# Calls, a doubled rest and a lag: three small moves in an attention and gated-MLP kernel

## The chip, the cores and the metric

The kernel runs on one core of one Trainium2 chip. The metric is the device time of one execution in microseconds (us), the median of several runs. TensorE (PE in the profile) multiplies matrices into PSUM, VectorE (DVE) and ScalarE (ACT) do the elementwise work, GpSimd (POOL) and SyncE (SP) mostly issue transfers (DMAs) here.

## The reference, cut to what matters

All numbers are 32-bit floats, with S = 2048 tokens and D = 576 features.

```python
qkv = layernorm(x) @ wqkv                  # 32 heads of 18 features, split into q, k, v
for each token s, head h:                  # a window of 8 keys, two tokens apart
    att = softmax(q[s] . k[s - 2*w] * 18**-0.5 for w in range(8))   # masked below token 0
    o[s] = sum(att[w] * v[s - 2*w])
h = x + o @ wo
g, u = layernorm(h) @ w_gate, layernorm(h) @ w_up       # 4608 features each
out = h + (sigmoid(g) * u) @ w_down
```

## The kernel before, in words

**Blocks and groups.** The tokens are cut in four blocks of 512: block b holds the even (0, 1) or odd (2, 3) tokens of one half of the sequence. A block is four tiles of 128 tokens (NS = 4). The heads are cut in four groups g of eight heads (CG = 144 features). Most products are done in split precision: an operand is split into a high half (copied by ACT with rounding, line 104) and a low half (the difference, taken by VectorE, line 105), and three products of halves are added (`tok_major`, `prod`).

**The 576 features** are handled as four chunks of 128 and a rest of 64. The rest is doubled: columns 512 to 575 are copied to columns 576 to 639 (DX = 640), the doubled rest is transposed as one tile of 128 (`tr_rest`, line 150), and `split_rest` makes the upper 64 rows the low half (lines 108 and 109). A plain tile without that copy of the rest has D = 576 columns. The copy is called the twin here.

**QKV calls.** `qkv(b, g, ...)` is one call: four passes, one a tile, of 14 matmuls each (lines 157 to 160), each evicted by ACT (line 403). After the last pass ACT issues three stores: q, k and v of that block and group go to device memory (lines 407 and 409), and `emitted` notes (b, g). The split weights of a group, `w[g]`, live in two buffers (tag "qw"): `w[2]` takes the place of `w[0]`, `w[3]` that of `w[1]`, so the splits of `w[3]` have to wait for the last call that uses `w[1]`. `heads(order, ws, n)` runs a list of calls, and between two passes it lets the attention advance by n steps.

**Attention units.** `attention(at, b, g, o)` is one unit, all on VectorE but for one exponential: SP loads q, the keys kw and the values vw with their windows (lines 176 to 178), then come two multiplies of 128x2304 (line 189) and two reductions (line 193) for the logits, the softmax (lines 198 to 207), and two more multiplies with their additions (lines 215 to 226). A unit ends with o for its group: for block 0 it lies in a tile in the core, for blocks 1 to 3 POOL stores it to device memory (`oscr`, line 228), and with the last group a second, small store adds the twin (line 230). `att_all` runs the units of blocks 0 and 1 in the order (0,0), (0,1), (1,0), (0,2), (0,3), (1,1), (1,2), (1,3); a unit waits until its call has been emitted. After (0, 3) four copies make the twin of block 0's o (line 428) and `ready` is set.

**The front.** `proj_j` is the output projection of one tile: it transposes o (lines 146 and 150), splits it, multiplies by wo, adds h (line 262), normalizes and transposes again. `front` does this for block 0, in between the last calls, (2, 3) and (3, 3): after two passes of (2, 3) come its first two steps, the transposes and splits of all four tiles. The blocks 1, 2 and 3 get the same later, in the background of the MLP (`proj_scr`), with o loaded back from device memory (`oj`, `load_j`, line 956) in tiles of DX columns.

**The MLP.** A loop over weight blocks (`items`) does the gate and up products, for block 0 first alone (12 items, "std") and then for two blocks at a time with seven products in place of eight ("pair"), and the down products (lines 864 and 926). Background work (`bg_step`) is stepped in between, and a queue of down units is stepped by `units`. The attention of blocks 2 and 3 is such background work.

**The tail.** For the last weight blocks, `load_tails` loads the sums of the down products back from memory (lines 1232 and 1235), lets seven steps pass (`lag(7)`), and adds three pairs of them on VectorE (line 1240), one in each of the next steps, each issued behind the last addition (`added[0]`) of the pair at work: s1 (line 825) before step 1, s3 (line 839) before step 4, s2 (line 844) before step 5.

**What sets the order.** Each engine runs its instructions in one fixed order. The build makes it from the order in which the program is written, a model of times, and priorities: `high_priority` moves what is in its block forward. `tc.issue_after(x)` puts the instructions of its block behind x on x's engine. A tile's buffer is reused when those who read it are done.

Of the kernel before, what the change touches and what calls it, by code (L numbers as in the profile page):

```python
# [15 lines left out]
F32 = mybir.dt.float32  # L16
F32R = mybir.dt.float32r
AF = mybir.ActivationFunctionType
ALU = mybir.AluOpType
# [41 lines left out]
def kernel(ctx, tc, x, wqkv, wo, wmlp, out):  # L61
# [29 lines left out]
    qscr = [[dr.tile([P, NS * CG], F32, name=f"q{b}_{g}") for g in range(NG)] for b in range(4)]  # L91
    oscr = {b: dr.tile([P, NS, DX], F32, name=f"o{b}") for b in (1, 2, 3)}
    hacc = [dr.tile([P, NS, D], F32, name=f"h{b}") for b in range(2)]
# [6 lines left out]

    splits = []

    def split(hi, lo, src):
# [3 lines left out]
    def split_rest(t, src):  # L107
        act.activation(t, src, AF.Copy)
        dve.tensor_tensor(t[64:128], src[64:128], f32(t[64:128]), ALU.subtract)  # L109

# [57 lines left out]
    def attention(at, b, g, o):  # L168
# [17 lines left out]
        for u in range(2):  # L186
            us = slice(2 * u, 2 * u + 2)
            pr = at.tile([P, 2, W, CG], F32, name="pr")
            dve.tensor_tensor(pr, both(kw, u), q[:, us].unsqueeze(2).broadcast_to([P, 2, W, CG]),  # L189
                              ALU.mult)  # L190
            yield
            yield
            dve.tensor_reduce(lg[:, us].rearrange("p j w h -> p (j w h)"),  # L193
                              pr.rearrange("p j w (h d) -> p (j w h) d", d=DH),
                              AX.X, ALU.add)
            yield
# [30 lines left out]
        if spill:  # L227
            pool.dma_start(oscr[b][:, :, g * CG:(g + 1) * CG], o)
            if g == NG - 1:
                pool.dma_start(oscr[b][:, :, D:DX], o[:, :, CG - DR:CG])  # L230

# [14 lines left out]

    def proj_j(bank, t, wos, th, tl, xn_tile, put, order=(0, 1)):
        oj = t[0]
        pv = tr_main(bank(), oj)
        with tc.high_priority(HI):  # L250
            split(th[:, 0:4], tl, pv)
        yield
# [160 lines left out]
    o = None  # L413
    emitted = set()
    ready = []
    passes = []

    def att_all():
        nonlocal o
        for b, g in ((0, 0), (0, 1), (1, 0), (0, 2), (0, 3), (1, 1), (1, 2), (1, 3)):  # L420
            while (b, g) not in emitted:
                yield
            if o is None:
                o = tok_tile()
            yield from attention(at, b, g, None if b else o[:, :, g * CG:(g + 1) * CG])
            if (b, g) == (0, 3):
                for j in range(NS):
                    dve.tensor_copy(o[:, j, D:DX], o[:, j, DM:D])
                ready.append(b)

# [154 lines left out]
    pads(2)  # L585
    heads(((2, 1), (3, 1)), w, 2)
    w.append(qkv_w(3, wr))
    pads(3)
    h = load_x(0)
    wos = [None, wo_w(1, swo.tile([P, 2, 5, DH2], F32R, tag="wo", name="wo1"))]  # L590
    heads(((0, 2), (0, 3), (1, 2), (2, 2), (3, 2)), w, 2)
    wos[0] = wo_w(0, saw.tile([P, 2, 5, DH2], F32R, tag="qw", bufs=2, name="wow"))
# [61 lines left out]
    with tc.issue_after(getattr(last, "ins", last)):  # L654
        for _ in range(2):
            next(fr)
    for b in (2, 3):
        for j, _ in enumerate(more if b == 2 else qkv(b, 3, T[b], w[3])):
# [294 lines left out]
    def load_j(pj, b, j, i):  # L953
        e, hf = BLOCKS[b]
        t = pj.tile([P, D if i else DX], F32, bufs=NS, name="hj" if i else "oj")
        paced(t, (xv[e, hf] if i else oscr[b])[:, j])
        return t

    def proj_scr(pj, b, raw, wos, ins=None, after=None):
# [3 lines left out]
        def tile_j(t, j):  # L963
# [11 lines left out]

            yield from proj_j(bg_bank, t, wos, th[:, :, js], tl[:, :, js], lambda: t[0], put, (1, 0))

# [244 lines left out]
    def load_tails():  # L1222
# [145 lines left out]
```

## Time and profile before

| what | us |
|---|---|
| median of 3 runs | 1581.41 (1580.72 to 1584.34) |
| the profiled execution | 1584.01 |
| its span, from the first to the last instruction | 1582.2 |
| TensorE busy | 1551.0 |
| VectorE busy | 1255.2 |
| ACT busy | 879.2 |
| POOL busy | 199.9 |

A line of the timeline reads: start, duration, engine, line of the kernel, operation, tile written <- tiles read, shapes, count, and in brackets the idle time of the engine before it with what ended it. A line of the waits reads: who waited for whom, us in total, times, the longest. A line of the chain of work that ended last reads: start, duration, what. A line of the windows reads: the window, its length, busy time and count of TensorE's matmuls, its weight loads, VectorE, ACT and POOL, then the clock granted to TensorE as a share of full speed, the busy share of the DMA engines and GB/s.

### The profile page before, as it was taken

The page shows a single profiled execution, that of the slowest core. Times are in us where ns is not written, and L with a number is a line of the kernel's source. Part 1 is how long each engine was busy: PE and PEld are TensorE (multiplying, and loading weights), DVE is VectorE, ACT ScalarE, POOL GpSimd, SP SyncE. Part 2 cuts the span into 40 slices and gives each one's busy share as a digit, 9 for nine tenths or more (in the row PEclk, how much of TensorE's full clock was granted, in tenths as well). Part 3 has the DMA queues.
Part 4 walks back from the last instruction along what each step waited for, and adds up shares of the span by engine and source line. Part 5 has one row for each costly group of instructions (what it writes and reads, how often), then busy time and mean ns, then how long its engine had stood idle before and what let it go on. Part 6 is the DMA issues. An engine that isn't in the chain of part 4 may idle for free.

```text
span 1582.2 us, 22347 instructions
## 1 busy us (share of the span) xinstructions
PE 1551.0 (98%) x8520; PEld 1377.3 (87%) x8520; DVE 1255.2 (79%) x1883; ACT 879.2 (56%) x1584; POOL 199.9 (13%) x249
## 2 busy tenths in 40 slices
PE   8999999999999999999999999999999999999998
PEld 7999888887888888888888888888888888888887
DVE  6998999969999999999426588866777776677755
ACT  6632244435555645566542355766777766777660
POOL 2300000020000010000101010112112112111210
PEclk9999999999999999999999999999999999999999
DMA  8646445365566677664683524999899989999983
GB/s 284 215 168 220 179 185 190 108 235 183 133 167 170 164 176 192 157 162 109 161 242 125 181 81 126 193 181 177 170 180 186 173 173 181 173 173 186 181 169 120
DMA packets 77147, 273.95 MB, mean 173 GB/s; under 512 B 8336, under 2 KB 14224, under 8 KB 76144
## 3 DMA queue, kind: packets, MB, share of 16 engines
q0 software_dynamic: 28192, 107.29, 37.5%
q1 hardware_dynamic: 41216, 145.11, 27.2%
q10 hardware_dynamic: 7632, 20.12, 3.3%
q8 instruction: 66, 1.08, 0.3%
q14 instruction: 41, 0.34, 0.1%
HBM read 143.98 MB, written 130.87 MB: 174 GB/s over the span
## 4 chain that ended last, share of the span: by engine, by line
PE 58%; issue 16%; DVE 11%; DMA 8%; POOL 4%; ACT 2%; SPq 0%; ACTq 0%; POOLq 0%; DVEq 0%
PE b L746 27%; PE dp L864 13%; PE dp L926 6%; PE b L753 5%; PE acc L157 4%; POOL h L935 3%; DMA wg<-in_wmlp_dram 3%; DVE pr L189 2%; DVE pr L215 1%; DVE lg L193 1%; DVE w L105 1%; DVE pr L221 1%; PE b L157 1%; PE bgp L157 1%; DMA x<-tok 1%
## 5 line engine op out<-in xcount | busy, mean ns | idle before, releaser
L746 PE MATMUL b<-tl,w 128*128 128x512 f32 x1704 | 432.6, 393 | 5.1 <-ACT s L820 3.2
L746 PEld LDWEIGHTS b<-tl,w 128*128 128x128 f32 x1704 | 307.9, 188 | 63.6 <-ACT s L820 4.7
L746 PE MATMUL b<-th,w 128*128 128x512 f32 x1344 | 346.2, 392 | 1.5 <-DVE s L839 1.5
L746 PEld LDWEIGHTS b<-th,w 128*128 128x128 f32 x1344 | 244.8, 188 | 46.5 <-DVE s L839 1.9
L932 ACT ACTIVATE ev<-dp 128x576 f32<-128x576 f32 x224 | 144.7, 646 | 63.2 <-PE dp L926 58.9
L753 PE MATMUL b<-th,w 128*128 128x512 f32 x568 | 175.7, 390 | 0.0
L104 ACT ACTIVATE w<-wg 128x384 fp32r<-128x384 f32 (+1 forms) x186 | 110.8, 601 | 111.1 <-PE b L753 48.8
L935 POOL DMA_DIRECT2D h<-ev x128 | 110.0, 860 | 458.6 <-ACT ev L932 444.7
L157 PE MATMUL acc<-qw,th 128*128 128x432 f32 x512 | 154.3, 362 | 2.5 <-DVE th L109 2.3
L105 DVE TENSOR_TENSOR w<-wg,w 128x640 fp32r<-128x640 f32 (+1 forms) x186 | 120.8, 656 | 41.3 <-ACT w L104 41.1
L105 DVE TENSOR_TENSOR w<-tw,w 128x512 fp32r<-128x512 f32 x120 | 82.6, 688 | 82.1 <-ACT w L104 81.5
L753 PEld LDWEIGHTS b<-th,w 128*128 128x128 f32 x568 | 106.5, 188 | 23.2
L864 PE MATMUL dp<-d,h1h 128*128 128x288 f32 x640 | 119.9, 297 | 0.0
L864 PE MATMUL dp<-d,h0h 128*128 128x288 f32 x608 | 114.1, 297 | 0.8 <-DVE tail L874 0.8
L872 ACT ACTIVATE stage<-dp 128x576 f32<-128x576 f32 x104 | 66.9, 645 | 70.1 <-PE dp L864 69.8
L157 PEld LDWEIGHTS acc<-qw,th 128*128 128x128 f32 x512 | 96.6, 189 | 8.4 <-DVE th L109 3.5
L864 PEld LDWEIGHTS dp<-d,h1h 128*128 128x128 f32 x640 | 99.7, 190 | 3.0
L104 ACT ACTIVATE w<-tw 128x512 fp32r<-128x512 f32 x120 | 75.4, 628 | 46.5 <-PE b L746 40.0
L864 PEld LDWEIGHTS dp<-d,h0h 128*128 128x128 f32 x608 | 95.1, 190 | 4.3 <-DVE tail L874 1.0
L157 PE MATMUL acc<-qw,tl 128*128 128x432 f32 x256 | 92.6, 362 | 0.1
L189 DVE TENSOR_TENSOR pr<-kw,q 128x2304 f32<-128x2304 f32 x32 | 81.8, 2556 | 8.8 <-DMA kw<-k 8.7
L880 POOL DMA_DIRECT2D h<-stage x26 | 31.0, 1194 | 436.3 <-ACT stage L872 350.1
(310 smaller groups left out, 2955.5 us busy)
## 6 DMA issues: line engine op xcount, KB each, us to landing
h<-ev POOLq DMA_DIRECT2D x96, 576.0 KB, 7.1
wg<-in_wmlp_dram SPq DMA_DIRECT2D x47, 928.0 KB, 5.9
h<-stage POOLq DMA_DIRECT2D x26, 1152.0 KB, 9.5
wg<-in_wmlp_dram SPq DMA_DIRECT2D x36, 640.0 KB, 4.3
kw<-k SPq DMA_DIRECT2D x16, 792.0 KB, 5.2
vw<-v SPq DMA_DIRECT2D x16, 792.0 KB, 4.3
wd<-in_wmlp_dram SPq DMA_DIRECT2D x18, 576.0 KB, 7.4
h<-ev POOLq DMA_DIRECT2D x32, 288.0 KB, 6.9
```

The lines of the kernel that those rows point to most:

```text
L104: act.activation(hi, src, AF.Copy)
L105: splits.append(dve.tensor_tensor(lo, src, f32(hi), ALU.subtract))
L157: pe.matmul(ps[:, :n], a[:, c, js], m[:, c], start=k == 0, stop=False)
L189: dve.tensor_tensor(pr, both(kw, u), q[:, us].unsqueeze(2).broadcast_to([P, 2, W, CG]), ALU.mult)
L746: pe.matmul(ps, wt[:, a, k0 + c], xx[:, m + c], start=first and k == 0, stop=k == 5, skip_group_check=True)
L753: pe.matmul(ps, wt[:, a, k0], xx[:, 4], start=False, stop=a == 1, skip_group_check=True)
L864: pe.matmul(ps[:, i, :DH2], a[:, js], d[:, m, i * DH2:(i + 1) * DH2], start=k == 0, stop=k == n)
L872: act.activation(hv, ps, AF.Copy)
L880: pool.dma_start(hacc[b], hs, accum_op=ALU.add, max_dma_last_dim=8 * D)
L926: pe.matmul(ps[:, i, :DH2], a[x][:, js], m[y], start=k in (0, 1, 3) and q == 0, stop=q == 2, skip_group_check=True)
L932: act.activation(hs[:, k % 2], ps[:, :, :DH2], AF.Copy)
L935: pool.dma_start(hsev[:, u, k0:k + 1], hs[:, :k + 1 - k0], accum_op=ALU.add, max_dma_last_dim=8 * D)
```

## The change

It has three parts.

- **Calls and order at the front.** The calls after (2, 0) and (3, 0) ran in the order (2,1), (3,1), (0,2), (0,3), (1,2), (2,2), (3,2). Now they run (2,1), (0,2), (3,1), then three passes of (1,2), then (0,3), the last pass of (1,2), (2,2), (3,2). The twin of block 0's o is one copy of four rows of 64. The first multiply of unit (1, 1) is issued behind that copy. The unit then stands after its first reduction until the front's first two steps are written (`gate`), and its second multiply is issued behind the last rest split of the front (`rests`).
- **The doubled rest.** `oscr` has D columns, the small store is gone, and oj is loaded without its twin; `proj_j` makes the twin by a copy on ACT for blocks 1 to 3 (`twin=True`), written after the four main transposes and ahead of their split.
- **The tail.** `lag(7)` is `lag(8)`.

```diff
-    oscr = {b: dr.tile([P, NS, DX], F32, name=f"o{b}") for b in (1, 2, 3)}
+    oscr = {b: dr.tile([P, NS, D], F32, name=f"o{b}") for b in (1, 2, 3)}
...
     def split_rest(t, src):
         act.activation(t, src, AF.Copy)
-        dve.tensor_tensor(t[64:128], src[64:128], f32(t[64:128]), ALU.subtract)
+        m = dve.tensor_tensor(t[64:128], src[64:128], f32(t[64:128]), ALU.subtract)
+        rests.append(getattr(m, "ins", m))
...
-            dve.tensor_tensor(pr, both(kw, u), q[:, us].unsqueeze(2).broadcast_to([P, 2, W, CG]),
-                              ALU.mult)
+            with ExitStack() as way:
+                if (b, g, u) == (1, 1, 0):
+                    way.enter_context(tc.issue_after(ready[0]))
+                elif (b, g, u) == (1, 1, 1):
+                    way.enter_context(tc.issue_after(rests[-1]))
+                dve.tensor_tensor(pr, both(kw, u),
+                                  q[:, us].unsqueeze(2).broadcast_to([P, 2, W, CG]), ALU.mult)
...
             pool.dma_start(oscr[b][:, :, g * CG:(g + 1) * CG], o)
-            if g == NG - 1:
-                pool.dma_start(oscr[b][:, :, D:DX], o[:, :, CG - DR:CG])
...
-    def proj_j(bank, t, wos, th, tl, xn_tile, put, order=(0, 1)):
+    def proj_j(bank, t, wos, th, tl, xn_tile, put, order=(0, 1), twin=False):
         oj = t[0]
         pv = tr_main(bank(), oj)
         with tc.high_priority(HI):
+            if twin:
+                act.activation(oj[:, D:DX], oj[:, DM:D], AF.Copy)
             split(th[:, 0:4], tl, pv)
...
-            yield from attention(at, b, g, None if b else o[:, :, g * CG:(g + 1) * CG])
+            unit = attention(at, b, g, None if b else o[:, :, g * CG:(g + 1) * CG])
+            if (b, g) == (1, 1):
+                for _ in range(3):
+                    next(unit)
+                    yield
+                while not gate:
+                    yield
+            yield from unit
             if (b, g) == (0, 3):
-                for j in range(NS):
-                    dve.tensor_copy(o[:, j, D:DX], o[:, j, DM:D])
-                ready.append(b)
+                twin = dve.tensor_copy(o[:, :, D:DX], o[:, :, DM:D])
+                ready.append(getattr(twin, "ins", twin))
...
-    heads(((2, 1), (3, 1)), w, 2)
+    heads(((2, 1), (0, 2), (3, 1)), w, 2)
     w.append(qkv_w(3, wr))
...
-    heads(((0, 2), (0, 3), (1, 2), (2, 2), (3, 2)), w, 2)
+    first = qkv(1, 2, T[1], w[2])
+    for _ in range(3):
+        next(first)
+        step(ag, 2)
+    heads(((0, 3),), w, 2)
+    for _ in first:
+        step(ag, 2)
+    heads(((2, 2), (3, 2)), w, 2)
...
     with tc.issue_after(getattr(last, "ins", last)):
         for _ in range(2):
             next(fr)
+    gate.append(True)
...
-        paced(t, (xv[e, hf] if i else oscr[b])[:, j])
+        paced(t[:, :D], (xv[e, hf] if i else oscr[b])[:, j])
...
-        yield from lag(7)
+        yield from lag(8)
```

More of the change, by code (lines that the diff above doesn't have):

```diff
@@ L101 @@
     splits = []
+    rests = []
     def split(hi, lo, src):
@@ L414 @@
     emitted = set()
+    gate = []
     ready = []
@@ L974, in put @@
                 act.activation(raw[:, cs, js], pv, AF.Copy)
-            yield from proj_j(bg_bank, t, wos, th[:, :, js], tl[:, :, js], lambda: t[0], put, (1, 0))
+            yield from proj_j(bg_bank, t, wos, th[:, :, js], tl[:, :, js], lambda: t[0], put, (1, 0),
+                              True)
         todo = []
```

## The prediction

> **What bounds the kernel now.** I read the page first (busy shares), then TensorE's list of waits, then the timelines of TensorE and VectorE around each wait that the change touches, then the windows with the granted clock.
>
> ```profile
> PE 1551.0 (98%) x8520; PEld 1377.3 (87%) x8520; DVE 1255.2 (79%) x1883; ACT 879.2 (56%) x1584; POOL 199.9 (13%) x249
> ```
>
> TensorE is busy for 1551.0 of 1582.2 us and the change adds and removes no matmul, so only two things can move the time: the 31 us in which TensorE stands, and the clock that it is granted while it works. The waits say whom it stands for:
>
> ```profile
> PE b L146 <- DMA oj<-o: 4.2, 1, 4.2
> ...
> PE b L746 <- DVE s L839: 1.5, 1, 1.5
> ```
>
> The longest after the start-up is one transpose that waits for the attention result of block 1 to come back from memory; another is a wait for a VectorE addition near the end. Two more lie where the front (block 0's output projection) begins:
>
> ```profile
> 181.79 0.33 PE L150 MATMUL mm<-ident,tok 128*128 128x128 f32 x1 [1.70 <-DVE tok L428]
> ...
> 185.30 0.46 PE L157 MATMUL acc<-qw,th 128*128 128x432 f32 x1 [1.65 <-DVE th L109]
> ```
>
> The change has a part for each of these. The profiled execution took 1584.01 us, 1.8 beside its span, and lies 2.6 above the median of the runs, 1581.41; I make the sum in the profile and take it off the median.
>
> **Part 1: the call (0, 2) goes ahead of (3, 1), the twin is one copy ahead of the next unit, the splits go ahead of its second half.**
>
> ```profile
> 113.38 2.68 DVE L105 TENSOR_TENSOR qw<-h,qw 128x432 fp32r<-128x432 f32 x5
> ...
> 128.47 2.56 DVE L189 TENSOR_TENSOR pr<-kw,q 128x2304 f32<-128x2304 f32 x1 [4.78 <-DMA kw<-k]
> ...
> 152.69 2.55 DVE L189 TENSOR_TENSOR pr<-kw,q 128x2304 f32<-128x2304 f32 x1
> ...
> 178.78 2.55 DVE L189 TENSOR_TENSOR pr<-kw,q 128x2304 f32<-128x2304 f32 x1
> 181.25 0.49 DVE L428 COPY tok<-tok 128x64 f32<-128x64 f32 x4
> 181.65 2.55 DVE L193 TENSOR_REDUCE lg<-pr 128x128 f32<-128x2304 f32 x1
> ```
>
> These are the first multiplies of units (0, 2), (0, 3) and (1, 1), and the four copies that make block 0's o ready. VectorE works nearly without a break from 128.47; the one real hole is the 4.78 us before it, in which it waits for the keys of (0, 2). When they come is set by the call on TensorE:
>
> ```profile
> 113.66 2.35 PE acc L157 x12
> ...
> 116.40 2.35 PE acc L157 x12
> ```
>
> A pass takes 116.40 - 113.66 = 2.74 us, a call of four 10.96. The last pass of (0, 2) starts at 116.40 and its keys let VectorE go 12.07 later. One call earlier that is 117.5, before VectorE has finished (1, 0) at 123.7, so the 4.78 goes. With the call move its evictions, its three stores on ACT's queue and its three loads on SP's. These loads wait for the stores and for free buffers, and what SP has behind them at this place is the load for weight block 1 of the MLP, used only after the front; I cost this at nothing, under 5 us of cover.
>
> Against that, (0, 3) is emitted three passes (8.22 us) later. Its last pass starts at 116.40 + 10.96 + 8.22 = 135.58, its keys by the same 12.07 are there at 147.65, and VectorE wants them at 152.69 - 4.78 = 147.91. The cover is 0.3 us; a miss delays o one for one, and o has room, as follows. The splits of w[3] need the slot of w[1], now held by (3, 1) until 119.1 instead of 108.2. Their low halves ended at 116.06, 7.9 after the slot; that makes 127.0, and the first pass of (0, 3) starts at 116.40 + 10.96 = 127.36. That cover, too, is 0.4, and a miss stalls TensorE itself (a rival below).
>
> If both hold, o is done at 178.78 - 4.78 = 174.0. The twin comes straight behind as one copy (0.5 at most, by the four together), so at 174.5; TensorE asks for it at 181.79 - 1.70 = 180.09. The first wait goes, with 5.6 to spare. The new waits order VectorE only: behind the twin stand the multiply and reduce of (1, 1), 2.55 each, done by 179.6, and behind the splits stands the second multiply, for which only the same unit waits. Before, the reduce held the splits until 181.65 + 2.55 = 184.20 and TensorE went on 1.1 later. Now they start with the first high half, about 180.6 (an estimate: half a us after 180.09), and release TensorE at 181.7 to 182.4; it runs out of transposes at 185.30 - 1.65 - 1.70 = 181.95. Gain 185.30 - 182.3 = 3.0, between 1.7 (the first wait alone) and 3.35. All that follows on both engines moves with it.
>
> **Part 2: block 1's result without the doubled rest.**
>
> ```profile
> 308.83 0.63 POOL o L228
> 309.46 6.85 DMA o<-kw
> ```
>
> ```profile
> o<-kw POOLq DMA_DIRECT2D x1, 288.0 KB, 4.5
> ```
>
> ```profile
> 316.44 1.75 SPq L707 DMA_DIRECT2D oj<-o  x4
> ```
>
> The main store lands at 308.83 + 4.5 = 313.3, the small second one at 309.46 + 6.85 = 316.3, and the load of oj goes off right behind that one. Without it the load goes 3.0 earlier, and the 4.23 shrinks to 1.2. Bounds: 4.23 if the store lands faster alone; 2.2 if the load, now beside the weight load that SP issued ahead of it, takes one us longer. POOL loses three such issues; blocks 2 and 3 hide theirs. In exchange ACT makes the twin, twelve times:
>
> ```profile
> 61.38 0.25 ACT L142 ACTIVATE tok<-tok 128x64 f32<-128x64 f32 x1
> ```
>
> That is 3.0 us of an engine 56% busy, each beside TensorE's four main transposes, so mostly hidden. I charge 0.3, between 0 and 3.0.
>
> **The clock behind that wait.**
>
> ```profile
> 389.40:396.00 6.60, 4.23 (x19) 3.11 (x17) 3.35 (x6) 4.63 (x9) 0.00 (x0) 1.00 0.01 2
> 317.73:324.55 6.82, 5.13 (x22) 5.08 (x23) 1.50 (x3) 1.55 (x3) 0.00 (x0) 0.50 0.97 365
> 836.55:839.96 3.41, 3.41 (x16) 3.41 (x15) 1.31 (x3) 1.33 (x2) 0.00 (x0) 0.50 0.99 394
> ```
>
> ```profile
> 319.42 1.11 PE L146 MATMUL b<-ident,oj 128*128 128x128 f32 x4 [4.23 <-DMA oj<-o]
> ...
> 393.31 1.43 PE L746 MATMUL b<-tl,w 128*128 128x512 f32 x5 [2.37 <-ACT s L820]
> ...
> 835.96 0.66 PE L146 MATMUL b<-ident,oj 128*128 128x128 f32 x4 [1.95 <-DVE tl L105]
> ```
>
> ```profile
> 179.00:182.00 3.00, 1.30 (x10) 0.99 (x9) 3.00 (x6) 1.03 (x2) 0.00 (x0) 1.00 1.00 351
> 182.00:186.00 4.00, 2.35 (x19) 2.09 (x17) 3.91 (x7) 2.36 (x7) 0.00 (x0) 1.00 1.04 430
> ```
>
> The granted clock (the third figure from the end of a window's row) is 0.50 from 317.73 to 324.55, and TensorE works 5.13 us in it: 2.56 lost. A wait of 1.95 was followed by 3.41 us at half clock too, one of 2.37 by none, and the two of 1.7 at the front by none. So 1.2 should keep the clock, and 2.56 comes back, less what the later oj tiles then cost:
>
> ```profile
> DMA to landing us min/median/max: 2.9/3.5/5.1
> ```
>
> The last tile lands up to 2.2 later after its issue than the first, which the half clock hid; I take off 0.7, an estimate. Gain 1.9, between 0 and 2.56.
>
> [...]
>
> **Part 3: `lag(8)`.**
>
> ```profile
> 1546.95 1.36 DVE L1240 TENSOR_TENSOR tail<-tail,more 128x1152 f32<-128x1152 f32 x1 [5.02 <-DMA tail<-h]
> 1548.22 0.68 DVE L839 TENSOR_TENSOR s<-s,b 128x512 f32<-128x512 f32 x1
> 1549.88 1.36 DVE L1240 TENSOR_TENSOR tail<-tail,more 128x1152 f32<-128x1152 f32 x1 [0.98 <-DMA tail<-h]
> 1551.16 0.68 DVE L844 TENSOR_TENSOR s<-s,b 128x512 f32<-128x512 f32 x1
> ```
>
> ```profile
> 1555.03 0.53 PE L864 MATMUL dp<-d,h0h 128*128 128x288 f32 x2 [0.78 <-DVE tail L874]
> ```
>
> VectorE stood for a load in front of L839, for which TensorE then waited 1.5. One step later the first addition stands behind L839 and the second behind L844. The 1.5 goes; but the second addition still cannot start before its load, 1549.88, and only L844 (0.6) leaves the chain from there to the L874 that ends TensorE's next wait. So at least 0.6 is gained and at most 1.49 + 0.78 = 2.27, if the third addition also falls behind that L874. I take 1.2.
>
> **Sum:** -3.0 - 3.0 - 1.9 - 1.2 + 0.3 = -8.8. The profile would go from 1584.0 to 1575.2, the median from 1581.4 to **1572.6**.
>
> **Rivals.**
> (a) *The load takes the wait's place.* The oj load meets the weight load, the wait stays near 2 us and the clock halves as at 836.55: part 2 gives 2.2, the clock 0. Sum -6.1, 1575.3. For it: both transfers are in flight; against: one is nearly landed.
> (b) *w[3] comes late.* If VectorE places a 2.56 multiply ahead of the low halves, the cover of 0.4 fails, TensorE stalls about 2.6 in (0, 3), and the front gains nothing. Sum -8.8 + 3.0 + 2.6 = -3.2, 1578.2. Against it: the splits have the higher priority in the program.
> (c) *Slower: ACT stands on a twin.* The twin waits for its oj load in ACT's order, and sigmoids and weight splits queue behind it. At the eight tiles of blocks 2 and 3 such a hold would reach TensorE as ACT's lateness did at 393.31, 2.37 each: 1572.6 + 19.0 = 1591.6. It decides from 8.8 / 8 = 1.1 us a twin. Against it: those loads are issued several steps before use, and the wait at 835.96 was for VectorE, not for the load. [...]
> (d) *It does not do what it says:* the program is ordered anew and other waits of 1 to 2.4 us, as at 393.31 or 835.96, grow by what is gained: 1581.
>
> **How the numbers follow.** Forecast 0.58, (a) 0.18, (b) 0.10, (c) 0.09, (d) 0.05. All gains at their upper ends give -3.35 - 4.23 - 2.56 - 2.27 = -12.4, 1569.0; the other end is (b), 1578.2. Outside lie (c), (d) and a little of the edges. About 0.2% (3.2 us) can be told from no change, so (b) lies on that bound and I halve it: faster 0.58 + 0.18 + 0.05 = 0.81, within 0.10, slower 0.09.
>
> **What would show it.** Right: VectorE's wait for kw of some 5 us gone near 121; the twin as one copy near 174; no wait at L150 of the front; one POOL store per unit and an oj wait of 1 to 2 us near 313; no stretch at 0.50 there; L839 ahead of the first L1240. Wrong: a TensorE wait for qw near 127 (b), a half clock near 316 (a), or TensorE waiting for ACT near the twins in the 800s (c). A median above 1578.2 would mean that the gains were paid back elsewhere.

## The result, and the profile after

The changed kernel takes 1588.54 us, the median of 10 runs (1584.7 to 1593.58), beside 1582.49 for the kernel before in the same comparison. The ratio is 1.0044, with a 95% interval of 1.0031 to 1.0058: slower by about 7 us (the medians lie 6.1 apart), where 8.8 less had been forecast. Single executions spread by some 5 us to either side of a median, so a verdict below is a ratio with its interval, and a trace, which shows one execution, is read for its mechanism. The profiled execution took 1590.32, its span 1588.5. Line numbers are now those of the changed kernel (the transposes L146 and L150 are L148 and L152, the L864 of the down product is L886, L746 is L768); an experiment's rows have those of its own kernel, a few lines off.

The busy line of the page, of the kernel after, says that no engine has got more to do:

```profile
PE 1554.3 (98%) x8520; PEld 1379.0 (87%) x8520; DVE 1254.9 (79%) x1880; ACT 882.4 (56%) x1596; POOL 198.1 (12%) x246
```

ACT has 12 instructions more, the twins, and 3.2 us; POOL three fewer. What changed is whom TensorE waits for (its list of waits, after):

```profile
PE b L768 <- ACT tl L105: 7.9, 2, 6.9
...
PE dp L886 <- ACT stage L894: 3.7, 1, 3.7
PE b L148 <- DVE tl L106: 2.0, 1, 2.0
PE dp L886 <- DVE tail L896: 2.0, 1, 2.0
```

The 4.2 for o is gone from the list, and the first two entries are new. The same waits in TensorE's timeline, with the places that the prediction named:

```profile
128.74 0.46 PE L159 MATMUL acc<-qw,th 128*128 128x432 f32 x1 [1.02 <-DVE qw L106]
...
183.14 0.33 PE L152 MATMUL acc<-ident,tok 128*128 128x128 f32 x1 [0.26 <-DVE th L110]
...
329.31 0.66 PE L148 MATMUL b<-ident,oj 128*128 128x128 f32 x4
...
368.29 0.80 PE L768 MATMUL b<-tl,w 128*128 128x512 f32 x1 [6.92 <-ACT tl L105]
370.03 1.22 PE L768 MATMUL b<-tl,w 128*128 128x512 f32 x2 [0.94 <-ACT tl L105]
...
810.50 0.85 PE L886 MATMUL dp<-d,h1h 128*128 128x288 f32 x2 [3.74 <-ACT stage L894]
...
1559.63 0.53 PE L886 MATMUL dp<-d,h0h 128*128 128x288 f32 x2 [1.95 <-DVE tail L896]
```

At the front the two waits of 1.70 and 1.65 are down to 0.26, and the transposes of o (329.31) follow without a wait. Behind 368.29, 810.50 and 1559.63 the clock is halved (windows of the kernel after; the 0.50 is the granted clock as a share of full speed):

```profile
365.42:375.66 10.24, 6.43 (x14) 4.73 (x15) 9.33 (x9) 5.66 (x8) 2.07 (x3) 0.50 1.05 301
809.15:815.98 6.83, 5.48 (x18) 5.00 (x19) 1.49 (x3) 2.70 (x6) 0.00 (x0) 0.50 0.01 3
1560.08:1563.49 3.41, 3.41 (x16) 3.41 (x15) 0.92 (x2) 0.00 (x0) 0.00 (x0) 0.50 0.00 0
```

Both kernels have 8520 matmuls, so the start of the n-th (counted from 0) can be compared in the two timelines. The difference says where the time went:

| matmul | start before | start after | after - before | what lies between |
|---|---|---|---|---|
| 640 | 129.98 | 131.18 | +1.20 | the wait for qw, w[3] |
| 1120 | 218.92 | 217.43 | -1.49 | the front: -2.7 |
| 1600 | 311.46 | 309.74 | -1.72 | |
| 1920 | 370.8 | 360.3 | -10.5 | no wait for o, no half clock behind it; 2.3 is another mix of matmuls |
| 2000 | 386.68 | 389.81 | +3.13 | 6.92 + 0.94 and a longer half clock |
| 2080 | 405.34 | 405.54 | +0.20 | before's wait at 393.31 |
| 4240 | 798.77 | 797.96 | -0.81 | |
| 4320 | 812.98 | 818.68 | +5.70 | the wait behind the twins, with its half clock: +6.5 |
| 8240 | 1529.68 | 1534.89 | +5.21 | |
| 8480 | 1572.19 | 1578.25 | +6.06 | the tail: +0.85 |

At the 1920th the changed kernel has done 24 of the 128x512 matmuls fewer and 24 of the shorter 128x288 ones more, which by their usual distances of 0.228 and 0.132 us is 2.3 us of the -10.5; in the other rows looked at (1600, 2000, 2080 and 4240) the mix is the same.

### The profile page after: what moved, and what is told of

Its sections match the earlier page's. It is cut to its first block, busy times and chain, and to the rows that moved or that the text cites. A ratio compares the mean times of both kernels' runs of the same rounds, so it can differ in the third digit from the quotient of the medians.

```text
span 1588.5 us, 22342 instructions
## 1 busy us (share of the span) xinstructions
PE 1554.3 (98%) x8520; PEld 1379.0 (87%) x8520; DVE 1254.9 (79%) x1880; ACT 882.4 (56%) x1596; POOL 198.1 (12%) x246
## 4 chain that ended last, share of the span: by engine, by line
PE 56%; issue 17%; DVE 13%; DMA 8%; POOL 4%; ACT 2%; ACTq 0%; SPq 0%; POOLq 0%; DVEq 0%
PE b L768 26%; PE dp L886 10%; PE dp L948 6%; PE b L775 5%; PE acc L159 4%; POOL h L957 3%; DMA wg<-in_wmlp_dram 3%; DVE pr L222 2%; DVE lg L200 2%; DMA oj<-o 2%; DVE pr L196 1%; DVE w L106 1%; PE b L159 1%; PE bgp L159 1%; DVE s L788 1%
## 5 line engine op out<-in xcount | busy, mean ns | idle before, releaser
L768 PE MATMUL b<-tl,w 128*128 128x512 f32 x1704 | 436.6, 396 | 9.3 <-ACT tl L105 7.9
L768 PEld LDWEIGHTS b<-tl,w 128*128 128x128 f32 x1704 | 310.5, 189 | 69.2 <-ACT tl L105 8.8
L768 PE MATMUL b<-th,w 128*128 128x512 f32 x1344 | 345.8, 392 | 0.0
L768 PEld LDWEIGHTS b<-th,w 128*128 128x128 f32 x1344 | 245.2, 188 | 44.7
L886 PE MATMUL dp<-d,h1h 128*128 128x288 f32 x640 | 119.8, 297 | 3.7 <-ACT stage L894 3.7
L886 PE MATMUL dp<-d,h0h 128*128 128x288 f32 x608 | 114.1, 297 | 2.0 <-DVE tail L896 2.0
L886 PEld LDWEIGHTS dp<-d,h1h 128*128 128x128 f32 x640 | 99.5, 190 | 7.0 <-ACT stage L894 4.2
L894 ACT ACTIVATE stage<-dp 128x576 f32<-128x576 f32 x104 | 66.7, 645 | 67.7 <-PE dp L886 67.5
L886 PEld LDWEIGHTS dp<-d,h0h 128*128 128x128 f32 x608 | 95.5, 191 | 5.4 <-DVE tail L896 2.2
```

What stands on the lines that cost most here:

```text
L768: pe.matmul(ps, wt[:, a, k0 + c], xx[:, m + c], start=first and k == 0, stop=k == 5, skip_group_check=True)
L886: pe.matmul(ps[:, i, :DH2], a[:, js], d[:, m, i * DH2:(i + 1) * DH2], start=k == 0, stop=k == n)
L894: act.activation(hv, ps, AF.Copy)
```

## What the two traces suggest, and the theories

**The loss near 368.** POOL's row for the store of block 1's last unit, (1, 3), stood at 308.83; it now reads

```profile
321.83 0.71 POOL L235 DMA_DIRECT2D o<-kw  x1 [43.07 <-DVE kw L233]
```

13.0 later. Counted in the program before, unit (1, 1) has 15 of its 16 steps taken when the MLP starts; in the changed kernel it has 9, because the steps that it is offered while it stands are lost. Its second half comes behind the splits of the MLP's first weights, and VectorE stands in front of these (VectorE's timeline, after):

```profile
220.39 0.82 DVE L106 TENSOR_TENSOR wf<-h,wf 128x640 fp32r<-128x640 f32 x1 [3.74 <-ACT wf L105]
...
226.35 0.69 DVE L788 TENSOR_TENSOR s<-s,b 128x512 f32<-128x512 f32 x1 [1.15 <-ACT s L815]
226.96 2.55 DVE L222 TENSOR_TENSOR pr<-vw,lg 128x2304 f32<-128x2304 f32 x1
```

The L222 at 226.96 is the unit's second multiply with the values. Before, it ran in that hole:

```profile
214.30 2.55 DVE L215 TENSOR_TENSOR pr<-vw,lg 128x2304 f32<-128x2304 f32 x1
```

In windows from 200 to 240 VectorE (the third busy time) worked 37.56 us before and works 30.25 after. Before, with a second row for the whole stage:

```profile
200.00:240.00 40.00, 39.26 (x202) 33.76 (x201) 37.56 (x63) 18.84 (x43) 3.22 (x5) 1.00 0.52 192
130.00:370.00 240.00, 230.14 (x1278) 207.48 (x1277) 214.58 (x297) 93.49 (x179) 15.15 (x24) 0.99 0.49 175
```

After:

```profile
200.00:240.00 40.00, 38.16 (x193) 32.48 (x192) 30.25 (x57) 19.91 (x44) 3.61 (x5) 1.00 0.55 201
```

The 7.3 us less are about the 7.86 that TensorE stands at 368 and 370. **Theory 1:** the stand of (1, 1) costs by the work that VectorE does not do there. Rivals: the loss comes from another part; or the work costs wherever it is put, since VectorE is short of time in this whole stage.

**The loss at 810.** ACT's timeline, after:

```profile
805.72 0.26 ACT L257 ACTIVATE oj<-oj 128x64 f32<-128x64 f32 x1 [2.17 <-DMA oj<-o]
...
809.65 0.26 ACT L257 ACTIVATE oj<-oj 128x64 f32<-128x64 f32 x1 [3.68 <-DMA oj<-o]
809.82 1.17 ACT L894 ACTIVATE stage<-dp 128x576 f32<-128x576 f32 x2
```

Two twins stand in ACT's order ahead of their load, and the eviction L894, for which TensorE waits 3.74, stands behind the second. The transposes of their tiles start at 836.80 and the first split of these at 840.14, so ACT's order has the two twins 30 us ahead of the work that they belong to. **Theory 2:** the twin's place on ACT costs about 6.5. Rival: ACT is late there for another reason.

**The tail.** **Theory 3:** `lag(8)` costs. The rival is the forecast, a gain of 1.2.

## The experiments

All are timed against the kernel before (1580.67 to 1582.4 us over the comparisons); "ratio" is to it, in brackets the interval. Where an edit is on the changed kernel, its own 1.0044 is the mark. Two ratios that lie less than some 0.002 apart are not told apart by one pair.

**1. The lost steps given back in the last six passes of the front.**

```diff
                 next(fr, END)
-            step(ag, 1)
+            step(ag, 2)
```

> The changed kernel, with the attention stepped twice instead of once in each pass of the loop over the calls (2, 3) and (3, 3), which gives unit (1, 1) back the six steps that the gate took from it: 15 of its 16 are then written before the MLP, as before the change. Theory 1 (lost steps): block 1's last unit ends some 13 us later after the change, its projection and the operands of the pair items come late, and TensorE waits 6.9 + 0.9 us for them near 368 and loses 3.7 more to half clock. Then the 6.9 us wait goes, the store of block 1's o goes out near 305 to 308 again, and the time is 1588.5 - 11 = 1577.5, between 1575 and 1580. Theory 2 (only the twins on ACT cost): the wait near 368 has another cause and stays; the time stays within 2 of 1588.5.

Measured: 1593.85, ratio 1.0078 [1.0055, 1.0102], worse than the changed kernel. The wait of 6.92 is gone, but others took its place, the longest of them in the first items (TensorE's timeline):

```profile
240.82 0.61 PE L886 MATMUL dp<-df,h0h 128*128 128x288 f32 x1 [2.44 <-ACT h0h L105]
```

So the steps do decide over the wait near 368, but taking them there does not win the time back.

**2. Each twin behind its tile's main split.**

```diff
         with tc.high_priority(HI):
-            if twin:
-                act.activation(oj[:, D:DX], oj[:, DM:D], AF.Copy)
-            split(th[:, 0:4], tl, pv)
+            hi = split(th[:, 0:4], tl, pv)      # split returns its ACT copy
+            if twin:
+                with tc.issue_after(getattr(hi, "ins", hi)):
+                    act.activation(oj[:, D:DX], oj[:, DM:D], AF.Copy)
```

> The changed kernel, with ACT's twin copy issued behind the split of the same tile's main transposes instead of ahead of it, so that in ACT's order it can't stand in front of older work. Theory 2 (a twin waits for its load in ACT's order): the 3.7 us wait of TensorE for the eviction near 810 and the half clock after it go, 1588.5 - 6 = 1582.5, between 1580.5 and 1584; the waits near 368 stay at 6.9 + 0.9. Theory 1 (lost steps alone): the wait near 810 comes from the later background order and stays, 1588.5 within 2.

Measured: 1582.05, ratio 1.0004 [0.9991, 1.0017], against 1.0044: 0.4%, some 6.3 us. TensorE passes the place without a wait and at full clock:

```profile
809.95 0.42 PE L888 MATMUL dp<-d,h1h 128*128 128x288 f32 x2
```

Theory 2 held, and its size (6.5) too.

**3. Part 2 alone**, on the kernel before (the store and load of D columns, the twin on ACT ahead of the split).

> The kernel before, with the second part of the change alone (no stored twin, the copy on ACT). The prediction's sum: the wait for oj near 319 shrinks from 4.2 to 1.2 and its half clock goes, -4.6: 1582.5 - 4.6 = 1577.9. Theory 2: the same gain, but ACT stands on a twin near 800 and TensorE loses about 6 there: 1583.9, between 1582 and 1586. Under theory 1 there is no wait of several us near 365 in this kernel, since it has all its steps.

Measured: 1583.92, ratio 1.0018 [1.0005, 1.0031]. Its timeline has the forecast's gain and theory 2's loss side by side (TensorE, then ACT):

```profile
315.31 0.66 PE L146 MATMUL b<-ident,oj 128*128 128x128 f32 x4 [1.63 <-DMA oj<-o]
...
806.48 0.53 PE L864 MATMUL dp<-d,h1h 128*128 128x288 f32 x2 [1.81 <-ACT stage L872]
```

```profile
805.63 0.26 ACT L250 ACTIVATE oj<-oj 128x64 f32<-128x64 f32 x1 [3.66 <-DMA oj<-o]
```

The wait for o fell from 4.23 to 1.63, where the forecast said 1.2, and in this execution the half clock behind it went: the four transposes take 0.66 us, where they took 1.11 before (in that of experiment 7 it did not); another came behind a wait of 2.64 near 389. The ratio shows a small loss in place of the gain.

**4. `lag(8)` alone**, on the kernel before.

> The kernel before, with the third part alone, lag(8). The prediction: 1582.5 - 1.2 = 1581.3, with L839 no longer behind the first addition. Theory 3 (the wait only moves: the additions now hold the end of the pair and the first L874, and TensorE waits 2 us there, with half clock behind it): 1582.5 + 0.9 = 1583.4. Both lie inside 2 us of before, so the waits in the trace tell more than the time.

Measured: 1584.73, ratio 1.0021 [1.0004, 1.0038]. The wait for L839 is gone, but the one for the tail's addition has grown from 0.78 to 1.99 and has half a clock behind it:

```profile
1547.66 0.85 PE L864 MATMUL dp<-d,h0h 128*128 128x288 f32 x2 [1.99 <-DVE tail L874]
```

```profile
1547.63:1551.04 3.41, 3.38 (x14) 3.38 (x15) 0.73 (x2) 0.00 (x0) 0.00 (x0) 0.51 0.00 0
```

Up to the tail this program is that of before, and its trace shows how far two executions of the same work can lie apart: here the wait for o is 2.93 and the half clock behind it 3.41 us, where the trace of before has 4.23 and 6.83, and the 1920th matmul starts 4.7 us sooner.

**5. Part 1 alone**, on the kernel before (calls, one copy, the stand; the doubled rest and `lag(7)` as before).

> The kernel before with part 1 alone: the new order of the calls, the one copy for the twin of block 0 and the stand of unit (1, 1). The doubled rest and lag(7) are those of before. Theory 1 (the stand of unit (1, 1) takes its steps away, so block 1's last unit ends some 13 us later and the wait near 368 is part 1's own): if the three parts add up, part 1 is what the changed kernel has over before (1588.5 - 1582.4 = 6.1) less part 2 alone (1.5) and lag(8) alone (2.3), so 2.3: 1584.7, with a wait of several us behind the low halves of block 1's tiles near 365 to 370. Rival (the parts work on one another: that wait comes from the twins on ACT ahead of the split): no wait above 2 us there, the front's gain of 2 to 3 stays: 1579.9.

Measured: 1579.72, ratio 0.9998 [0.9988, 1.0009]. The ratio lies between the two expectations, but the mechanism is that of theory 1:

```profile
331.78 0.63 PE L148 MATMUL b<-ident,oj 128*128 128x128 f32 x4 [0.61 <-DMA oj<-o]
...
367.04 0.79 PE L768 MATMUL b<-tl,w 128*128 128x512 f32 x1 [5.87 <-ACT tl L105]
368.78 1.22 PE L768 MATMUL b<-tl,w 128*128 128x512 f32 x2 [0.94 <-ACT tl L105]
```

The wait near 368 is part 1's own. So is most of the vanished wait for o: with the doubled rest still there, 0.61 is left of 4.23, since the transposes of o now come 12 us later. What part 1 wins at the front and at o it pays at 367: against the trace of before it is 2.8 us ahead at the 1600th matmul and 0.65 behind at the 2000th. Behind that it is ahead again, by 5.4 at the 8480th, but 4.7 of that can be the executions' own (experiment 4), and the ratio shows nothing left.

**6. Part 1 alone, without the stand.**

```diff
-                elif (b, g, u) == (1, 1, 1):
-                    way.enter_context(tc.issue_after(rests[-1]))
...
-            if (b, g) == (1, 1):
-                for _ in range(3):
-                    next(unit)
-                    yield
-                while not gate:
-                    yield
```

> Part 1 alone again, but without its stand: unit (1, 1) does not stop after three steps and its second multiply is not held behind the last rest split. The order of the calls, the one copy and the first multiply behind that copy stay. 14 of the unit's 16 steps are then taken before the MLP, in place of 9. Theory 1: block 1's last unit ends within 3 us of before's 308.83 and the wait near 368 is under 1.5 us; the front keeps the 2.1 us that the changed kernel had gained by its 291st part of the work, so 1580.3. Rival (the front's gain comes from the stand, not from the order of the calls): the two front waits of 1.70 and 1.65 us come back and the time is before's, 1582.4.

Measured: 1585.09, ratio 1.0025 [1.0012, 1.0038]. The rival was right that the front's gain comes from the stand, but the time is over before's: the unit ends in time (its store at 309.53), the wait near 368 is gone, and the front pays:

```profile
185.73 0.33 PE L152 MATMUL acc<-ident,tok 128*128 128x128 f32 x1 [3.69 <-DVE th L110]
```

**7. Part 2 alone with the twin behind the split**, and **8. the changed kernel without the stand, with the twin behind and `lag(7)`**.

> The kernel before with part 2 alone, and each twin on ACT issued behind the split of its tile's four main chunks in place of ahead of it. Theory 2 (a twin ahead of the split makes ACT stand on a load): part 2 alone cost 1.5 us with the twin ahead; behind the split the 1.81 us wait for ACT's stage eviction near 806 goes and what is left is the load, which starts earlier without the small store: 1581.9. Rival (part 2 costs by something else, such as the narrower loads or the order that the build makes): 1583.9, as with the twin ahead.

> The changed kernel with three edits: no stand of unit (1, 1), each twin behind its tile's main split, and lag(7) in the tail. If theories 1 to 3 add up: before's 1582.4, less 2.1 at the front, less 0.5 for part 2 with the twin behind: 1579.8, and faster than before. Rival (the gain at the front is lost wherever the attention's work is put, since VectorE gives it back in the first items of the MLP): 1582.5, no different from before.

Measured: 1580.37, ratio 1.0002 [0.9989, 1.0014], and 1584.11, ratio 1.0013 [1.0001, 1.0025]. Part 2 shows no gain even where its twin is harmless. In this trace (7) its wait for o is 1.95, and 3.41 us at half clock follow:

```profile
314.00 0.33 PE L147 MATMUL b<-ident,oj 128*128 128x128 f32 x1 [1.95 <-DMA oj<-o]
```

In 8 the front's wait is 4.64, where 6 had 3.69. The sum of theories 1 to 3 failed.

**9. The twin behind and `lag(7)`.**

> The changed kernel with each twin behind its tile's main split, and lag(7) in place of lag(8). If the tail adds to the rest as it did alone (lag(8) alone was slower by a ratio of 1.0021, some 3.3 us), this lies 3.3 us under the kernel with the twin behind alone (1.0004 of before): 0.9983 of before, 1578.7. Rival (the additions of the tail come late in either case, since the other parts move them too): 1581.9.

Measured: 1582.16, ratio 1.0015 [1.0004, 1.0025], no better than with `lag(8)` (1.0004). The rival was right.

**10. The reload of block 0's normalized x earlier, in the changed kernel, and 11. that with the twin behind and `lag(7)`.**

```diff
+        with sb_pool("pw", "right") as pw:      # holds wow, then ar0 in its place
...
+                    if n == 37:                 # behind the last product of block 1
+                        a0 = pw.tile([P, 2 * 5 * DH2], F32, tag="wow", bufs=1, name="ar0")
+                        a0 = a0[:, :5 * TB].rearrange("p (c n) -> p c n", c=5)
+                        pool.dma_start(a0, xscr[0])
```

> The changed kernel with one edit: the reload of block 0's normalized x (ar0) takes the place of the output weights (wow), which are read for the last time at the last product, and no longer a place that comes free with the last transposes of block 1. It can then be issued some 3.3 us earlier (by part 1 alone: 353.02, the last addition of a product, against 356.31, the issue). Theory 1 (the late last unit of block 1 costs by way of this reload, which lands 8.3 us after its issue): the waits of 6.92 and 0.94 us near 368 shrink by 3.3 in all and the half clock behind them from 10.24 us to 3.41 us, worth 3.4 more: 1588.5 - 6.7 = 1581.8. Rival (the reload is only the last of several that come late together, such as ACT's normalized rows of block 1): no more than 1 us: 1587.5.

> The three mends at once: each twin behind its tile's main split, lag(7), and the earlier reload of block 0's x. If each is worth what it is worth alone: 1578.7 for the first two, less 6.7: 1572.0, faster than before. Rival (the reload is not what comes last): 1578.0.

Measured: 1586.36, ratio 1.0035 [1.0022, 1.0049], and 1580.13, ratio 0.9995 [0.9982, 1.0008]. The two waits near 368, 7.86 together, became one of 5.71, and the half clock behind it 6.83 us in place of 10.24, though the medians show only 0.1 to 0.2%:

```profile
367.29 0.80 PE L768 MATMUL b<-tl,w 128*128 128x512 f32 x1 [5.71 <-ACT tl L105]
```

The reload is issued at 352.94 in place of 357.61, and VectorE no longer stands there (its L290 starts at 364.92 without idle time ahead of it, in place of 365.92 with 2.28): what comes last now is its own queue. Both sides were half right.

**12. The steps given back in the MLP's items 1 to 3** (with the twin behind and `lag(7)`): two more steps an item.

> Each twin behind its tile's main split, lag(7), and the attention's lost steps given back in the MLP: two more steps in each of the items 1, 2 and 3 (places 2 and 5), so that unit (1, 3) ends in the fifth item as before. Theory 1: the waits near 368 and the half clock behind them go, worth 8.4 us in the trace of part 1 alone (from -10.7 to -2.3 against before), and the wait for the load of o comes back in part, up to 1.6: 1578.7 - 8.4 + 1.6 = 1571.9. Rival (VectorE has no room in these items either, as it had none in the last calls): new waits for the splits of the hidden rows between 240 and 330, and 1580.0 or more.

Measured: 1583.74, ratio 1.0018 [1.0006, 1.0031]. Unit (1, 3) is stored at 322.21, no sooner than without them (320.61 in experiment 9), and the wait is 6.11. The steps are offered after the hole at 216 to 227, when VectorE is full again (12.81 us busy in the 13 from 227 to 240, 3.65 in the 11 before).

**13 to 16. The six steps taken right behind the front**, ahead of the splits of the first weights: in the changed kernel with the twin behind (13), with `lag(7)` too (14), in part 1 alone (15), and with the earlier reload besides the twin and `lag(7)` (16).

```diff
     with tc.high_priority(HI):
         drain(fr)
+    step(ag, 6)
```

> The changed kernel with each twin behind its tile's main split, and the six lost steps of unit (1, 1) taken between the front's last row and the first split of the MLP's weights. Theory 1b (part 1 leaves VectorE idle where it had been busy: 30.25 us busy between 200 and 240 in the changed kernel against 37.56 before, and these 7.3 us are missing near 368): VectorE is again over 36 us busy there, unit (1, 3) ends near 310, the waits near 368 (6.04 + 0.94 with the twin behind) fall under 2 and the half clock behind them goes, some 9 less; the wait for the load of o comes back with up to 3. So 1.0004 of before becomes 0.997: 1576. Rival (the attention's work costs wherever it is put, since VectorE is short of time from 130 to 370 and has to do the front's splits too): 1.000 or more, 1581.5.

> The same with lag(7). If the tail adds as lag(8) did alone (ratio 1.0021): 0.995, 1573. If it adds as it did together with the twin behind (lag(7) there was no better: 1.0015 against 1.0004): 0.997 to 0.998, 1577.

> The kernel before with part 1 alone (no part 2, lag(7)) and the six steps taken behind the front. Theory 1b: part 1 alone was 0.9998 of before with waits of 5.87 and 0.94 us near 368 and 6.83 us of half clock; without them some 9 less, and up to 3 back for the load of o: 0.996, 1575. Rival: 0.9998 or more, 1581.

> The twin behind, lag(7), the six steps behind the front and the earlier reload of block 0's x. With the waits near 368 already gone the reload is worth nothing more by theory 1b: as the kernel with lag(7) and the steps, 0.997. Rival (the reload is worth 0.2%, as it was without the steps: 0.9995 against 1.0015): 0.995.

Measured: 1586.45, ratio 1.0023 [1.0009, 1.0037]; 1586.79, 1.0028 [1.0015, 1.0042]; 1584.65, 1.0018 [1.0001, 1.0034]; 1584.15, 1.0012 [0.9997, 1.0027]. Each is slower than the same kernel without the steps. In 13 what theory 1 says of VectorE came true: it is busy for 34.94 us between 200 and 240, the second multiply is back in the hole, and unit (1, 3) is stored at 311.16 (VectorE's and POOL's timelines):

```profile
213.67 2.56 DVE L223 TENSOR_TENSOR pr<-vw,lg 128x2304 f32<-128x2304 f32 x1
```

```profile
311.16 0.71 POOL L236 DMA_DIRECT2D o<-kw  x1 [44.14 <-DVE kw L234]
```

No wait is left near 368. But TensorE's list of waits has others; in the first 500 us the longest are near 240, 319, 394 and 452:

```profile
PE b L771 <- ACT s L845: 4.0, 4, 2.9
PE dp L889 <- ACT h0h L105: 3.2, 2, 2.5
...
PE b L771 <- ACT s L855: 2.2, 3, 1.6
...
PE b L149 <- DMA oj<-o: 1.5, 1, 1.5
```

So the wait near 368 comes from the work left undone between 200 and 240: shown. And doing it there costs as much or more, in all four pairs: the rival holds too, though which of the new waits is the price was not tested one by one.

**17. Part 1 alone with the earlier reload, and 18. the changed kernel with the twin behind and the earlier reload, `lag(8)` kept.**

> The kernel before with part 1 alone and the earlier reload of block 0's x. If the reload is worth what it was worth in the changed kernel (1.0035 against 1.0044, and 0.9995 against 1.0015 with the other two mends), 0.1 to 0.2%, this is 0.998 to 0.999 of before and the fastest of all: 1579. Rival (VectorE is the bound there, and the order that its work takes around the reload decides): 0.9998, as part 1 alone.

> The changed kernel with each twin behind its main split and the earlier reload, and lag(8) left as it is. Theory 3 (lag(8) costs, 1.0021 alone): 0.9995, that of the same kernel with lag(7), times 1.0021: 1.0016 of before. Rival (the tail's cost hangs on where the chain of the last items stands, and lag(8) costs nothing in this one): 0.9995.

Measured: 1577.67, ratio 0.9976 [0.9967, 0.9985], and 1581.32, ratio 1.0001 [0.9990, 1.0012]. Number 17 is the one kernel that is faster than the kernel before, by 0.24%. The longer of its two waits there (TensorE's timeline) is smaller by 2.0 than that of part 1 alone:

```profile
365.88 0.80 PE L768 MATMUL b<-tl,w 128*128 128x512 f32 x1 [3.87 <-ACT tl L105]
```

Number 18 is the kernel of experiment 2 with the reload, 1.0001 after 1.0004: there the reload is worth nothing that shows.

**The pairs, read together.** Each mend was run in several surroundings, as ratio without and with it:

| mend | pairs |
|---|---|
| twin behind the split | 1.0044 to 1.0004; 1.0018 to 1.0002; 1.0035 to 1.0001 |
| earlier reload | 1.0044 to 1.0035; 1.0015 to 0.9995; 1.0028 to 1.0012; 0.9998 to 0.9976; 1.0004 to 1.0001 |
| steps given back behind the front | 1.0004 to 1.0023; 1.0015 to 1.0028; 0.9998 to 1.0018; 0.9995 to 1.0012 |
| the stand of (1, 1) taken away | 0.9998 to 1.0025; 1.0015 to 1.0013 |
| `lag(8)` in place of `lag(7)` | 1.0000 to 1.0021; 1.0015 to 1.0004; 0.9995 to 1.0001; 1.0028 to 1.0023 |

The first is worth 0.16 to 0.40%, the second 0.03 to 0.22%, the third costs 0.13 to 0.2%, each with one sign throughout. By their two intervals together, the pairs that are clear of noise by themselves are the first and third of the twin, the second and fourth of the reload and the first of the stand; for the other pairs of the first three rows it is the common sign that speaks. For the last two rows it depends on the surroundings; `lag(8)` is shown to cost only where it is the one change.

## Why the prediction was wrong, step by step

In the table of matmul starts the forecast's terms read as follows: the front -1.5 for -3.0, the load of o and its clock, with what followed near 368, +1.9 for -4.9, the twins +6.5 for +0.3, the tail +0.85 for -1.2; between these places lie another -1.7.

**Part 1, the front: right, with its rival in small.** Of -3.0, TensorE's timeline gave -2.7 between the 640th and the 1120th matmul; before that, w[3] came late by 1.02, the cover of 0.4 being too thin. It came late as rival (b) says, by unit work that VectorE takes ahead of the last low half (VectorE's timeline, after):

```profile
125.63 2.54 DVE L200 TENSOR_REDUCE lg<-pr 128x128 f32<-128x2304 f32 x1
128.09 0.60 DVE L106 TENSOR_TENSOR qw<-h,qw 128x432 fp32r<-128x432 f32 x1
```

Net of that the front gave -1.5.

**Part 1, "behind the splits stands the second multiply, for which only the same unit waits": the step that failed, and that took the gains away.** I asked who waits for the held instruction and stopped at its unit. Behind the unit stood the next two, block 1's o, its projection and the first products that use it. The steps that the unit lost while it stood were not counted at all. The hole that this left in VectorE is 7.3 us, the bill near 368 is 7.86 and a half clock. Part 1 alone, forecast at -3.0, gives 0.9998. The deeper miss is that the front's gain was taken as final. VectorE is busy for 214.58 of the 240 us from 130 to 370. Where the steps were given back (experiments 1 and 13 to 16) other waits came; where the unit did not stand (6 and 8) the front itself paid, with 3.69 and 4.64. That VectorE's fullness is the reason for all of these is argued from its busy time; no run made its work less. The page's 79% hid this: that share is a mean over the whole program. Rival (d), other waits that grow by what is gained, had 0.05 and describes part 1.

**Part 2, the load (-3.0) and the clock (-1.9): the mechanism right, the worth not.** Alone it brought the wait to 1.63 with the full clock in one trace and to 1.95 with 3.41 us at half clock in the other (experiments 3 and 7). In the changed kernel part 1 had already taken nearly all of that wait, so it could not be counted twice. Both terms were also read off one execution with a long wait: in experiment 4 the same code waited 2.93 and had half as much at half clock. From the 1600th to the 2080th matmul the changed kernel lost 1.9 where 4.9 were to be gained. With the twin harmless, part 2 alone is 1.0002 [0.9989, 1.0014].

**Part 2, the twins (+0.3): the second step that failed, and the one that made the kernel slower.** Rival (c), with 0.09, was what happened, at one place in place of eight. The dismissal, that "those loads are issued several steps before use", looked at the order of the program. ACT's own order has two of the twins 30 us ahead of their tiles' splits, and it is ACT's order that is carried out. The price was not 2.4 a tile but 6.5 once, with 6.83 us of half clock in it, in place of 0.3. Issuing the twin behind its split takes 0.40 of the 0.44% away: shown. ACT's row at 809.82 has an eviction that needs nothing of oj right behind the twin that had stood 3.68 for its load: in this trace what came later in ACT's order waited with the twin.

**Part 3 (-1.2): wrong in sign.** L844 (now L866) left the chain from the second addition on, but the third addition stays in it, now as the last thing ahead of the down product's own (VectorE's timeline, before and after):

```profile
1551.76 1.35 DVE L1240 TENSOR_TENSOR tail<-tail,more 128x1152 f32<-128x1152 f32 x1
...
1554.22 1.41 DVE L874 TENSOR_TENSOR tail<-tail,dp 128x576 f32<-128x576 f32 x2
```

```profile
1552.18 1.36 DVE L1263 TENSOR_TENSOR tail<-tail,more 128x1152 f32<-128x1152 f32 x1 [0.53 <-DMA tail<-h]
...
1557.56 1.35 DVE L1263 TENSOR_TENSOR tail<-tail,more 128x1152 f32<-128x1152 f32 x1
1558.83 1.41 DVE L896 TENSOR_TENSOR tail<-tail,dp 128x576 f32<-128x576 f32 x2
```

From the first addition to that of the down product it is 1558.83 - 1552.18 = 6.65, after 1554.22 - 1546.95 = 7.27 before, the 0.6 of the forecast's lower end. But two waits of 1.49 and 0.78 have become one of 1.95, and that one has 3.41 us at half clock behind it: +0.85 in all. Not every wait there has: in experiment 2 the wait at this place is 2.04, and the clock stays at 1.00 behind it. Alone `lag(8)` cost 0.21%; in three other surroundings it made no difference that shows. What decides there stays open.

**The clock term** rested on two rows, a wait of 1.95 with half a clock behind it and one of 2.37 with none, from which I took that a wait of 1.2 keeps the clock. That agrees with the full clock behind the 1.63 of experiment 3 and behind the 1.70 and 1.65 at the front of before (1.00 from 179 to 190), but by the length of the wait the two rows contradict each other. The last section has more such pairs; what tells them apart was not shown.

## What to carry to other kernels

When a change makes an engine wait, follow the held instruction to the last thing that needs it, and count the turns that its generator loses, not only the next consumer. A gain in front of a stage whose second engine is nearly full is a loan: look at the busy share of that engine in the window of the stage, and ask what it will be late with (here argued, from 214.58 of 240 us). A small copy that waits for a load belongs behind the work of its own tile on an engine that takes its work in order, as ACT did at 809.82, behind a twin that had stood 3.68 us; where it stands in the program says little, where it stands in that engine's order says all.

## What the runs showed of the hardware

In the trace of the changed kernel TensorE's clock is at 0.50 in the three stretches shown above, 10.24, 6.83 and 3.41 us long, and once more from 1587.4 to its end; in that of the kernel before for 6.83 us from 317.73, for 3.41 from 836.55, and from 1580.7 to its end. Among the waits of some 2 us in these traces the length did not tell whether such a stretch followed. In the changed kernel one of 1.95 ends at 1559.63, and 3.41 us at 0.50 follow from 1560.08; one of 1.99 ends at 841.69, and the clock is 1.00 from 837 to 845. Two other traces show the same. In experiment 9 a wait of 1.98 ends at 834.41, and the clock stays at 1.00 (TensorE's timeline, then two windows that meet within the wait):

```profile
834.41 0.44 PE L149 MATMUL b<-ident,oj 128*128 128x128 f32 x2 [1.98 <-DVE tl L106]
```

```profile
830.38:833.79 3.41, 2.05 (x11) 1.45 (x10) 2.80 (x6) 3.14 (x7) 0.00 (x0) 1.00 0.39 107
833.79:837.21 3.42, 2.80 (x22) 2.80 (x23) 2.48 (x4) 1.67 (x5) 0.00 (x0) 1.00 0.81 319
```

TensorE is busy for 2.05 us in the first window and for 2.80 in the second. In experiment 5 one of 1.94 ends at 832.47, with TensorE busy for 1.47 of the 3.41 us up to 832.56, and the next 3.41 run at half clock:

```profile
832.47 0.37 PE L148 MATMUL b<-ident,oj 128*128 128x128 f32 x1 [1.94 <-DVE tl L106]
```

```profile
829.15:832.56 3.41, 1.47 (x10) 1.01 (x9) 2.77 (x5) 3.33 (x7) 0.00 (x0) 1.00 0.26 58
832.56:835.97 3.41, 3.41 (x16) 3.41 (x17) 1.34 (x2) 1.12 (x2) 0.00 (x0) 0.51 0.98 391
```

Before's wait of 2.37 at 393.31, with 1.00 from 389.40 to 396.00, cost nothing beyond itself. What tells these waits apart was not tested by a run.

So of the waits of some 2 us in these traces some had 3.41 us at half clock behind them, which cost 1.7 us more (half of it) where TensorE was busy throughout, as from 1560.08, and some had none. Each execution has its mean granted clock on record: of the kernel before, nine with 0.993 took 1585.2 us in the mean, fifteen with 0.999 took 1578.4. Most of the spread of these executions goes with the clock, and a term read off one profiled execution carries its share of it.
